# Column-tiled matmuls and a weight matrix turned by DMA in a fused attention and feed-forward kernel

## The chip, the cores and the metric

The kernel runs on one core of one Trainium2 chip. The metric is device time in microseconds (us). The time of a kernel is the median of its runs. A run whose time is over 1.5% above the fastest run of the same kernel counts as slow and is left out of ratios. Times inside one execution come from its profile, in us from the start of its span.

## The reference

It is block-sparse attention, followed by a gated feed-forward network (FFN) without a nonlinearity.

```python
# q, k, v: (4 batches, 8 heads, 768, 64); blocks of 32; tokens = 4*768 = 3072
scores = q @ k.T / 8                      # masked by block: band, first/last block, 3 random blocks per row
attn   = softmax(where(mask, scores, -1e9)) @ v
x      = attn, heads side by side         # (3072, 512)
out    = ((x @ w1) * (x @ w2)) @ w3 @ w_out
# w1, w2: 512x1024; w3: 1024x1024; w_out: 1024x512
```

The kernel multiplies `w3 @ w_out` once (the "fold", tile `wp`) and uses the product for all tokens. The matmuls of this program, on TensorE (PE), take both operands with the summed index on their partitions, so the fold needs w3 turned (`w3t_sb`). Their results go to PSUM tiles, from which ACT (ScalarE) or DVE (VectorE) copies them. POOL (GpSimd) issues the loads, and SP (SyncE) the transposes by DMA.

## The kernel before

A small planner in the program puts the PE work into one fixed order ahead of time. It takes work from three queues: scores and q/k transposes (`qk`), attention output and row sums (`pv`), and everything else (`fill`: masks, fold, FFN). The `fill` queue is in order: what stands at its head blocks what stands behind it. These are the parts that matter here.

```python
# attention output o: four heads at once, each in its own 32 columns of the array
for g in range(4):
    i, h = divmod(g, 2)
    nc.tensor.matmul(acc["o"][32*g:32*g+32, part*QT:(part+1)*QT],
                     lhsT=vn[b, 2*Q+i][:, h, kc, 32*part:32*part+32],
                     rhs=e[:, g, k2*QT:(k2+1)*QT], ..., skip_group_check=True)
...
w3pool = pool("w3pool", 4)                       # four buffers for rows of w3
...
def fold_transpose(i, jh):                       # w3 turned on PE, then copied out of PSUM
    def emit(eng):
        tp = box["p"] = ps_f.tile([128, 4, 128], BF16, tag="f", name="w3p")
        for j in range(4):
            nc.tensor.transpose(tp[:, j, :],
                                w3_sb[i][:, (4*jh+j)*128:(4*jh+j+1)*128], ident)
    op, hold = f_op(0.23, emit, [w3_in[i]])
    w3_hold[i].frees = op
    hold.frees = either(0.42, lambda eng: copy(
        eng, w3t_sb[:, 4*jh:4*jh+4, i*128:(i+1)*128], box["p"]), [op])
...
def fold_mm(i, turned_at):                       # the fold: 128x128 stationary, 512 columns
    ...
    nc.tensor.matmul(box["p"], lhsT=w3t_sb[:, j, i*128:(i+1)*128],
                     rhs=wo_sb[:, j, :], start=j == 0, stop=j == NF-1)
...
def pa(f):                                       # first FFN product (pb is the same with w2)
    for c in range(4):
        nc.tensor.matmul(p, lhsT=w1_sb[:, c, f*128:(f+1)*128],
                         rhs=X[i][:, c, :], start=c == 0, stop=c == 3)
...
# q and k of batches 2 and 3 were already turned by DMA, in the middle of the kernel
nc.sync.dma_start_transpose(out=t[:, x, :].rearrange("r (c p) -> r c p", c=C),
                            in_=ns[x].rearrange("p c h d -> p (c h d)"))
```

The softmax here doesn't subtract the row's maximum and nothing guards it: scores larger than these inputs give would overflow.

## Time and profile before

| | before |
|---|---|
| time, median (range, runs) | 262.22 us (262.19 to 263.07, 3) |
| span of the profiled run | 260.9 us |
| PE busy | 248.4 us, 95% |
| first FFN matmul (`pa`) starts at | 61.8 us |
| PE instructions in program order | 5706 |

The lines below are from the profile's page of the kernel before. The first gives busy time, share of the span and instructions of each engine. The rows `PE` and `PEclk` cut the span into 40 slices and give tenths of busy time and of the full PE clock. The `q` lines are DMA queues: packets, megabytes, and the time of the packets as a share of 16 DMA engines. Queue q0 carries what POOL issues (the loads), q1 what SP issues, q8 fetches instructions.

```profile
PE 248.4 (95%) x2819; PEld 127.6 (49%) x2852; DVE 212.3 (81%) x250; ACT 198.8 (76%) x274; POOL 62.7 (24%) x100
...
PE   7999999999999999999999999999999999997994
...
PEclk9999999999999999999999999999999999999999
...
q1 hardware_dynamic: 17344, 10.88, 16.3%
q8 instruction: 22, 0.36, 0.6%
```

PE is busy in nearly every slice, and always at full clock. So PE bounds the kernel, and the questions are what its time consists of and whether the start, the only place with holes, can be packed more tightly.

The same run by stages: length, busy us and count of each engine, granted clock, DMA share (the time of all packets over that of 16 engines; packets overlap, so it can pass 1), and GB/s.

```profile
core 0: us, PE busy (x) PEld busy (x) DVE busy (x) ACT busy (x) POOL busy (x), PEclk, DMA share, GB/s
20.00:40.00 20.00, 19.00 (x271) 10.41 (x272) 16.26 (x22) 16.78 (x24) 5.90 (x10) 1.00 0.74 121
40.00:60.00 20.00, 18.27 (x259) 9.88 (x260) 16.55 (x19) 18.21 (x27) 16.27 (x27) 1.00 1.18 194
60.00:85.00 25.00, 24.52 (x322) 13.20 (x320) 21.52 (x27) 21.16 (x31) 14.39 (x19) 1.00 1.57 151
```

DMA is not full from 20 to 40 us. The waits of POOL show why: it can't start a load of w3 (`w_...`) before PE has turned an earlier part out of one of the four buffers (`w3p`). The columns are the total wait, how often, and the longest.

```profile
POOL w_722 L367 <- PE w3p L624: 5.3, 1, 5.3
POOL w_613 L367 <- PE w3p L624: 4.8, 1, 4.8
```

The timeline of PE in mid-kernel shows what a change of the array's mode costs. Columns: start, length of the group, the group.

```profile
150.15 0.61 PE L496 MATMUL s<-qkt 64*128 64x256 bf16 x8
150.69 1.50 PE L552 MATMUL o<-e,vn 128*32 128x256 bf16 x48
152.01 0.39 PE L564 MATMUL d<-sum,ones 128*32 128x256 bf16 x8
152.33 1.04 PE L661 MATMUL pa<-x,w_sb 128*128 128x512 bf16 x3
```

Ends are modelled, so starts are read. The row sums `d` (eight 32-column matmuls, two groups of 0.109 us) start at 152.01 and the 128-column `pa` starts 0.32 us later: about 0.1 us more than the streaming. That is a mode change. The step from `o` to `d`, both in 32 columns, has none: 48 matmuls are 12 groups, 12 x 0.109 = 1.31 us, and 152.01 - 150.69 = 1.32 us.

### The profile page before, as it was taken

Reading aid. Unit: us, or ns where it says so; the run is one execution under the profiler, and the core shown is the slowest. Engines: PE = TensorE matmul, PEld = TensorE weight load, DVE = VectorE, ACT = ScalarE, POOL = GpSimd, SP = SyncE. Lnnn points to the kernel's source line nnn. Section 1 sums busy time; section 2 is a strip of 40 time slices with the busy share of each in tenths; the row PEclk is TensorE's granted clock in tenths of the full one; section 3 lists DMA queues with packets and bytes.
Section 4 is the critical chain, followed back from the end, with each engine's and each line's share of the span. In section 5 each row is a group of like instructions: output and inputs, shape, how many; then the busy total and the mean of one; then the engine's idle time right before and its main releaser. Section 6 shows DMA issues by size and latency. Waiting matters only on the chain.

```text
span 260.9 us, 6636 instructions
## 1 busy us (share of the span) xinstructions
PE 248.4 (95%) x2819; PEld 127.6 (49%) x2852; DVE 212.3 (81%) x250; ACT 198.8 (76%) x274; POOL 62.7 (24%) x100
## 2 busy tenths in 40 slices
PE   7999999999999999999999999999999999997994
PEld 4444544554555445554555455545554555453441
DVE  5498789688977978999879988799988799945751
ACT  4789869988887898979899897999879989501000
POOL 8603138698356050009260000000000000000000
PEclk9999999999999999999999999999999999999999
DMA  6999639999989299119999000300002100031013
GB/s 222 163 200 202 104 52 172 206 204 184 164 124 140 60 173 130 33 33 101 164 214 171 3 1 17 124 25 3 0 3 93 72 4 0 3 121 43 0 41 121
DMA packets 53730, 25.34 MB, mean 97 GB/s; under 512 B 39236, under 2 KB 48708, under 8 KB 53700
## 3 DMA queue, kind: packets, MB, share of 16 engines
q0 software_dynamic: 36176, 13.90, 45.9%
q1 hardware_dynamic: 17344, 10.88, 16.3%
q8 instruction: 22, 0.36, 0.6%
q10 hardware_dynamic: 180, 0.13, 0.2%
q14 instruction: 8, 0.07, 0.1%
HBM read 29.36 MB, written 6.29 MB: 137 GB/s over the span
## 4 chain that ended last, share of the span: by engine, by line
PE 86%; DVE 5%; ACT 3%; DMA 2%; issue 2%; SPq 1%
PE pb L678 17%; PE po L699 16%; PE pa L661 16%; PE s L496 14%; PE o L552 13%; PE wp L642 4%; DMA raw<-in_k_dram 2%; DVE e L509 2%; PE d L564 2%; PE tp L399 2%; ACT e L504 2%; PE mp L476 1%; DVE x L604 1%; PE w3p L624 1%; SPq L251 1%
## 5 line engine op out<-in xcount | busy, mean ns | idle before, releaser
L504 ACT ACTIVATE e<-s 128x1024 bf16<-128x1024 f32 x144 | 141.5, 1028 | 14.8 <-PE s L496 14.8
L509 DVE TENSOR_TENSOR e<-e,mask 128x1920 bf16<-128x1920 bf16 x72 | 82.9, 1154 | 16.7 <-ACT e L504 15.7
L661 PE MATMUL pa<-x,w_sb 128*128 128x512 bf16 x175 | 47.6, 380 | 2.6 <-DVE x L604 1.3
L678 PE MATMUL pb<-x,w_sb 128*128 128x512 bf16 x190 | 49.3, 380 | 0.2
L496 PE MATMUL s<-qkt 64*128 64x256 bf16 x576 | 46.9, 279 | 0.7 <-ACT e L504 0.5
L699 PE MATMUL po<-wf_sb,h 128*128 128x512 bf16 x186 | 43.4, 380 | 0.7 <-issue 0.6
L552 PE MATMUL o<-e,vn 128*32 128x256 bf16 x1152 | 38.0, 278 | 1.2 <-DVE x L604 1.0
L496 PEld LDWEIGHTS <-qkt 64*128 64x128 bf16 x576 | 22.5, 96 | 30.7 <-issue 27.8
L684 DVE TENSOR_TENSOR h<-pb,a 128x512 bf16<-128x512 f32 x48 | 33.0, 687 | 4.5 <-PE pb L678 2.0
L552 PEld LDWEIGHTS <-vn 128*32 128x32 bf16 x1152 | 28.5, 98 | 9.6 <-issue 8.4
L535 DVE TENSOR_TENSOR sum<-e 128x2048 bf16<-128x2048 bf16 x24 | 29.3, 1222 | 0.7
L538 DVE TENSOR_TENSOR sum<-sum,e 128x2048 bf16<-128x2048 bf16 x24 | 29.3, 1222 | 0.5
L699 PEld LDWEIGHTS <-h 128*128 128x128 bf16 x192 | 17.6, 98 | 22.3 <-issue 3.2
L678 PEld LDWEIGHTS <-w_sb 128*128 128x128 bf16 x192 | 17.5, 98 | 22.1 <-issue 3.2
L661 PEld LDWEIGHTS <-w_sb 128*128 128x128 bf16 x192 | 16.7, 98 | 23.2 <-issue 6.7
L302 ACT CAST a<-pa 128x512 bf16<-128x512 f32 x36 | 21.2, 588 | 2.4 <-PE pa L661 1.5
L429 POOL DMA_DIRECT2D nt<-in_q_dram x16 | 13.2, 830 | 22.4 <-DMA qkt<-nt 14.6
L595 ACT ACTIVATE ln<-d 128x256 f32<-128x256 f32 x24 | 9.4, 392 | 11.9 <-PE d L564 11.9
L604 DVE TENSOR_TENSOR x<-o,rec 128x512 bf16<-128x512 f32 x24 | 16.4, 684 | 1.8 <-ACT rec L599 1.8
L336 POOL DMA_DIRECT2D vn<-in_v_dram x16 | 11.6, 727 | 24.2 <-PE o L552 20.4
L707 ACT COPY ob<-po 128x256 f32<-128x256 f32 x1 | 0.4, 372 | 21.3 <-PE po L699 21.3
L642 PE MATMUL wp<-wo_sb,w3t_sb 128*128 128x512 bf16 x56 | 15.6, 380 | 0.7 <-issue 0.5
(79 smaller groups left out, 170.0 us busy)
## 6 DMA issues: line engine op xcount, KB each, us to landing
out_dram<-ob SPq DMA_DIRECT2D x23, 256.0 KB, 2.0
vn<-in_v_dram POOLq DMA_DIRECT2D x16, 192.0 KB, 6.0
w_sb<-in_moe_w_dram POOLq DMA_DIRECT2D x16, 128.0 KB, 5.0
nt<-in_q_dram POOLq DMA_DIRECT2D x16, 96.0 KB, 4.5
nt<-in_k_dram POOLq DMA_DIRECT2D x16, 96.0 KB, 5.1
qn<-in_q_dram POOLq DMA_DIRECT2D x6, 192.0 KB, 6.1
kn<-in_k_dram POOLq DMA_DIRECT2D x6, 192.0 KB, 6.4
wo_sb<-in_moe_w_out_dram POOLq DMA_DIRECT2D x1, 1024.0 KB, 13.3
```

The lines of the kernel that those rows point to most:

```text
L302: (nc.scalar.copy if eng == "ACT" else nc.vector.tensor_copy)(dst, src)
L496: nc.tensor.matmul(s[:, h, k2 * QT:(k2 + 1) * QT], lhsT=qk[64 * h:64 * h + 64, 1, kc * 128:(kc + 1) * 128], rhs=qk[64 * h:64 * h + 64, 0, ...
L504: nc.scalar.activation(E[key][:, 2 * i:2 * i + 2, :], box["s"], AF.Exp, scale=1.0 / 8.0)
L509: nc.vector.tensor_tensor(e, e, m.to_broadcast((128, 4, 4, 120)), op=ALU.mult)
L535: nc.vector.tensor_tensor(box["sum"], E[es[0]], E[es[1]], op=ALU.add)
L538: nc.vector.tensor_tensor(box["sum"], box["sum"], E[es[2]], op=ALU.add)
L552: nc.tensor.matmul(acc["o"][32 * g:32 * g + 32, part * QT:(part + 1) * QT], lhsT=vn[b, 2 * Q + i][:, h, kc, 32 * part:32 * part + 32], rhs ...
L642: nc.tensor.matmul(box["p"], lhsT=w3t_sb[:, j, i * 128:(i + 1) * 128], rhs=wo_sb[:, j, :], start=j == 0, stop=j == NF - 1)
L661: nc.tensor.matmul(p, lhsT=w1_sb[:, c, f * 128:(f + 1) * 128], rhs=X[i][:, c, :], start=c == 0, stop=c == 3)
L678: nc.tensor.matmul(p, lhsT=w2_sb[:, c, f * 128:(f + 1) * 128], rhs=X[i][:, c, :], start=c == 0, stop=c == 3)
L684: nc.vector.tensor_tensor(box["h"][:, f, :], box["pb", f], box["a", f], op=ALU.mult)
L699: nc.tensor.matmul(box["o", n], lhsT=box["h"][:, f, n * 128:(n + 1) * 128], rhs=wf_sb[:, f, :], start=f == 0, stop=f == NF - 1)
```

## The change

The intent: let all PE work except scores and transposes run in one mode (four tiles of 32 columns), so that FFN, o and d can follow one another without a change; take the turning of w3 off PE, ACT and DVE and give it to the DMA; and pack the start more tightly (eight w3 buffers, FFN work in pieces of two instead of four matmuls, w1 and w2 loaded before the second batch, new planner constants). The core of the diff, with the cuts marked:

```diff
-    w3pool = pool("w3pool", 4)
-    nat = pool("nat", 4)
+    NW = 8
+    w3pool = pool("w3pool", NW)
+    nat = pool("nat", 8)
 ...
+    def quarters(to, lhsT, rhs, start, stop):
+        for g in range(4):
+            nc.tensor.matmul(to[32 * g:32 * g + 32], lhsT=lhsT[:, 32 * g:32 * g + 32], rhs=rhs,
+                             start=start, stop=stop, skip_group_check=True)
 ...
     def load_w3(lo, hi):
 ...
+            def turn(eng, i=i):
+                dma_at[0] += 1.0
+                nc.sync.dma_start_transpose(out=w3t_sb[:, :, i * 128:(i + 1) * 128], in_=w3_sb[i])
+            hold.frees = w3t_at[i] = plan.add(Op("SP", 1.7, turn, [w3_in[i]], lat=2.0))
 ...
-    def fold_transpose(i, jh):                   # all of it
 ...
+    STEP = 2
+    def chain(name, n, one, deps):               # fold, pa, pb and po all go through this
+        box, hold, ops = {}, Hold(), []
+        for lo in range(0, n, STEP):
+            def emit(eng, lo=lo):
+                if lo == 0:
+                    box["p"] = ps_f.tile([128, 512], F32, tag="f", name=name)
+                for j in range(lo, lo + STEP):
+                    lhsT, rhs = one(j)
+                    quarters(box["p"], lhsT, rhs, j == 0, j == n - 1)
+            ops.append(Op("PE", 0.215 * STEP, emit, deps(lo), [] if ops else [(F_SLOTS, hold)],
+                          "c", lat=0.2))
+        return ops, hold, box
 ...
     tps = {(0, pr): transposes(0, pr) for pr in range(4)}
-    load_pair(1, 0)
-    load_pair(1, 1)
     w1_in = load_w12(moe_w1, w1_sb)
     w2_in = load_w12(moe_w2, w2_sb)
-    load_pair(1, 2)
-    load_pair(1, 3)
+    for pr in range(4):
+        load_pair(1, pr)
+        plan.turn.extend(transposes(1, pr))
```

The mask matmuls also contract over 128 rows instead of 24, and the masks, o, d, fold and FFN share one mode name, "c", in the planner.

## The prediction

> **What bounds it now.** TensorE. The page has PE busy 95% of a 260.9 us span at full clock, DVE 81%, ACT 76%; the chain of waits is 86% PE. Starts of neighbouring matmuls in the timeline: 0.216 us per 128x512 FFN or fold matmul; 0.109 us per group of four 32-column matmuls over 256 columns (o, d) and per pair of scores; 0.056 us per w3 transpose. Times the counts in the program order: 219.7 us of streaming (576 FFN 124.3, 64 fold 13.8, o 31.4, scores 31.4, d 5.2, q/k transposes 7.4, w3 transposes 3.7, masks 2.3).
>
> On top come changes of array mode. FFN to scores starts 312 ns apart instead of 216, FFN to o 309, d to FFN or scores 205 instead of 107, scores to o 199: 93 to 99 ns each. The order has 206 changes: 20.0 us. The Trainium skill ("TensorEngine Tiling (Array Packing)", Key Properties) says that changing the mode drains TensorE; the trace agrees, with about 97 ns.
>
> First useful matmul 4.8 us, last one ends 3.6 us before the end. So 260.9 - 4.8 - 3.6 - 219.7 - 20.0 = 12.8 us are holes: about 10.6 before the first pa (61.8 us), 1.5 near 236 us (pa waits for the last x), almost none between 62 and 230.
>
> **What the change does.**
> - FFN, fold, masks as four 32-column matmuls: estimated from o's rate, 0.216 us per four of 512 columns: no change. PE instructions rise from 5706 to 9786, but eight per 0.216 us is half o's issue rate. The same page (Restrictions) says column tiling turns Fast Weight Load off; in the trace loads take 97 ns either way and hide.
> - FFN-o-d no longer switch mode. But scores stand between most of them: the order after has 175 changes, 31 fewer, 3.0 us; mostly early (68 to 46 before the first pa), in the middle only 136 to 129.
> - w3 by DMA: minus 64 PE transposes (3.7 us) and 16 evictions (0.42 us DVE, 0.59 us ACT). Plus eight DMA transposes; those of 192 KB took 1.2 to 1.4 us to issue and 2.5 to 7 us to land; estimate 1.7 us of all 16 engines and 6 us latency each. Eight w3 buffers end POOL's waits for w3p (12 us), with DMA half idle (28 to 40 us).
> - The last o and d now stand before 30 po matmuls: the hole near 236 us goes.
> - The first FFN may start after 29 score units, not 33; w1/w2 load before batch 1.
>
> **On the critical path.** All PE savings count, if holes do not grow: 4.8 + 216.0 + 17.0 + 3.6 + holes = 241.4 us + holes. Until the first pa, PE has 37 us of work after its start at 4.8, ACT is busy to about 49 us (29 x 1.03 plus copies), and w2 lands at 50 to 54 us (6.8 MB at the 0.2 MB/us seen, plus transposes). So 9 to 11 us of holes stay. Span 251.5, time about 1 more.
>
> **Prediction: 252.5 us, range 248.5 to 257.5.** Faster by over 2% 0.87, within 2% 0.12, slower 0.01.
>
> **What would show it.** FFN groups 0.216 us apart; d to pa without the 97 ns; first pa at 49 to 54 us; no hole before the last FFN; PE busy still 95%; ACT and DVE some 4 us less each.
>
> **What would make it wrong.** Four-tile groups slower than 0.216 us (1% is 1.4 us); instruction fetch falling behind; w3 transposes landing late, so that the in-order fold blocks the FFN behind it (5 us or more); or early loads so much better that holes fall to 5 us (247).

## The result and the profile after

| | before | after |
|---|---|---|
| time, median (range, runs) | 262.21 us (261.93 to 263.07, 4) | 292.13 us (288.43 to 295.39, 4, one of them slow) |
| ratio of fast runs | 1 | 1.109 (95% interval 1.098 to 1.120) |
| span of the profiled run | 260.9 us | 286.7 us |
| first `pa` at | 61.8 us | 84.7 us |
| mean granted PE clock | 0.998 | 0.944 |

A ratio here is the mean time of one kernel's fast runs over the mean of the other's in the same rounds, so it is not quite the ratio of the medians. The first three runs before are those of the table above. The kernel is 11% slower; 252.5 us was predicted. The profiled run (288.43 us) was a fast one.

The page after, the lines that answer to those before:

```profile
PE 251.8 (88%) x4892; PEld 133.8 (47%) x4892; DVE 211.8 (74%) x250; ACT 189.9 (66%) x259; POOL 62.9 (22%) x100
...
PE   6775714965589999999999999999999999999994
...
PEclk9795975797799999999999999999999999999998
...
q1 hardware_dynamic: 25792, 12.98, 28.7%
q8 instruction: 38, 0.62, 0.9%
```

The PE row has holes in its first twelve slices and is full from then on. The clock row has holes in the same place. Queue q1 carries 8448 packets and 2.10 MB more: the eight transposes of 256 KB, as 8192 packets of 256 bytes and 256 of 4 bytes. By stages, in the same columns as before:

```profile
20.00:40.00 20.00, 10.85 (x184) 5.06 (x176) 10.82 (x12) 6.88 (x10) 6.91 (x13) 0.82 1.25 178
40.00:60.00 20.00, 12.37 (x196) 5.96 (x200) 5.39 (x7) 7.19 (x10) 7.39 (x13) 0.67 1.26 110
60.00:85.00 25.00, 15.68 (x256) 7.50 (x252) 10.55 (x12) 12.06 (x18) 5.73 (x8) 0.86 1.30 128
85.00:150.00 65.00, 64.41 (x1304) 34.65 (x1300) 58.53 (x65) 60.40 (x84) 22.50 (x29) 1.00 1.05 95
```

Before 85 us PE, DVE and ACT do less than in the kernel before, PE partly at a lower clock. DMA is now full nearly all the time. It moves more from 20 to 40 us (178 GB/s instead of 121), but less from 40 to 60 us, 110 GB/s where it was 194, and this includes the w3 pieces. What PE waited for:

```profile
PE wp L299 <- DMA w3t_sb<-w_336: 9.9, 1, 9.9
PE wp L299 <- DMA w3t_sb<-w_511: 4.5, 1, 4.5
PE wp L299 <- DMA w3t_sb<-w_268: 4.5, 1, 4.5
...
PE wp L299 <- DMA w3t_sb<-w_546: 2.0, 1, 2.0
PE wp L299 <- DMA w3t_sb<-w_583: 1.9, 1, 1.9
```

Seven waits of the fold for a w3 transpose make 24.8 us (the five longest are shown). The timeline of PE shows the longest wait, and what such a wait costs afterwards:

```profile
35.56 1.48 PE L299 MATMUL wp<-wo_sb,w3t_sb 128*32 128x512 bf16 x24
46.93 1.04 PE L299 MATMUL wp<-wo_sb,w3t_sb 128*32 128x512 bf16 x8 [9.89 <-DMA w3t_sb<-w_336]
...
67.11 3.40 PE L299 MATMUL wp<-wo_sb,w3t_sb 128*32 128x512 bf16 x32 [4.50 <-DMA w3t_sb<-w_511]
70.44 0.61 PE L517 MATMUL s<-qkt 64*128 64x256 bf16 x8
```

The 32 matmuls from 67.11 us are eight groups of four. They take 70.44 - 67.11 = 3.33 us, where 8 x 0.216 = 1.73 us is the rate at full clock. The Trainium skill ("TensorE: Matmul & The Clock Gate", HAM oscillation) says that gaps of more than about 3.4 us make the clock fall to half; this trace agrees, with a group of four at 0.42 us after a gap of 4.5 us. But shorter gaps did it too: in this trace half clock also followed a gap of 2.0 us that began at 71.0 us, and in experiment 1 a stall of 2.0 us.

The DMA-issuing side, the timeline of SP. The length is that of the issuing instruction.

```profile
12.33 1.33 SPq L384 DMA_TRANSPOSE w3t_sb<-w_268  x1
19.77 1.89 SPq L384 DMA_TRANSPOSE w3t_sb<-w_313  x1
21.70 4.01 SPq L384 DMA_TRANSPOSE w3t_sb<-w_336  x1
28.68 11.82 SPq L384 DMA_TRANSPOSE w3t_sb<-w_440  x1
```

The transpose behind the 9.9 us wait was issued at 21.7 us and its user could start at 46.9 us: 25 us. Its successor kept SP busy for 11.8 us in issue alone.

What follows is, in its rates, what was predicted. The timeline of PE after 150 us:

```profile
151.16 0.62 PE L299 MATMUL po<-wf_sb,h 128*32 128x512 bf16 x8
151.60 1.49 PE L573 MATMUL o<-e,vn 128*32 128x256 bf16 x48
...
179.71 0.39 PE L585 MATMUL d<-sum,ones 128*32 128x256 bf16 x8
179.93 0.60 PE L299 MATMUL pb<-x,w_sb 128*32 128x512 bf16 x8
```

Two FFN groups of four tiles take 151.60 - 151.16 = 0.44 us, so a group costs 0.22 us, as much as one 128-column matmul before, and there is no extra step into `o`. From `d` to `pb` it is 0.22 us for two groups of 0.109 us: no mode change, where it was 0.32 us.

### The profile page after: what moved, and what is told of

It reads as the page before. It is cut to its first block, busy times and chain, and to the rows that moved or that the text cites. A ratio compares the mean times of both kernels' runs of the same rounds, so it can differ in the third digit from the quotient of the medians.

```text
span 286.7 us, 10729 instructions
## 1 busy us (share of the span) xinstructions
PE 251.8 (88%) x4892; PEld 133.8 (47%) x4892; DVE 211.8 (74%) x250; ACT 189.9 (66%) x259; POOL 62.9 (22%) x100
## 3 DMA queue, kind: packets, MB, share of 16 engines
q0 software_dynamic: 36176, 13.90, 48.9%
q1 hardware_dynamic: 25792, 12.98, 28.7%
## 4 chain that ended last, share of the span: by engine, by line
PE 69%; DMA 24%; POOL 3%; ACT 1%; DVE 1%; issue 1%; POOLq 0%
PE pb L299 15%; PE pa L299 15%; PE po L299 14%; PE s L517 11%; PE o L573 10%; DMA w3t_sb<-w_583 7%; DMA w_sb<-in_moe_w_dram 7%; DMA qn<-in_q_dram 5%; DMA w_511<-in_moe_w_dram 5%; PE d L585 2%; PE tp L416 1%; ACT e L525 1%; PE wp L299 1%; POOL vn L345 1%; POOL A L281 0%
## 5 line engine op out<-in xcount | busy, mean ns | idle before, releaser
L530 DVE TENSOR_TENSOR e<-e,mask 128x1920 bf16<-128x1920 bf16 x72 | 82.7, 1153 | 21.7 <-ACT e L525 21.4
L299 PEld LDWEIGHTS <-w_sb 128*32 128x32 bf16 x1536 | 37.5, 96 | 39.4 <-issue 6.5
L299 PE MATMUL pb<-x,w_sb 128*32 128x512 bf16 x768 | 51.8, 380 | 0.0
L299 PE MATMUL pa<-x,w_sb 128*32 128x512 bf16 x768 | 51.1, 380 | 0.0
L299 PE MATMUL po<-wf_sb,h 128*32 128x512 bf16 x768 | 45.2, 380 | 0.0
L299 PE MATMUL wp<-wo_sb,w3t_sb 128*32 128x512 bf16 x256 | 22.3, 493 | 24.8 <-DMA w3t_sb<-w_336 9.9
L573 PEld LDWEIGHTS <-vn 128*32 128x32 bf16 x1152 | 30.1, 99 | 7.6 <-issue 4.3
L299 PEld LDWEIGHTS <-h 128*32 128x32 bf16 x768 | 19.3, 97 | 20.0 <-issue 2.5
L299 PEld LDWEIGHTS <-w3t_sb 128*32 128x32 bf16 x256 | 6.9, 114 | 35.2 <-DMA w3t_sb<-w_336 10.4
L316 ACT CAST a<-pa 128x512 bf16<-128x512 f32 x33 | 19.5, 591 | 3.4 <-PE pa L299 3.3
## 6 DMA issues: line engine op xcount, KB each, us to landing
kn<-in_k_dram POOLq DMA_DIRECT2D x6, 192.0 KB, 14.3
```

The lines of the kernel that those rows point to most:

```text
L299: nc.tensor.matmul(to[32 * g:32 * g + 32], lhsT=lhsT[:, 32 * g:32 * g + 32], rhs=rhs, start=start, stop=stop, skip_group_check=True)
L316: (nc.scalar.copy if eng == "ACT" else nc.vector.tensor_copy)(dst, src)
L530: nc.vector.tensor_tensor(e, e, m.to_broadcast((128, 4, 4, 120)), op=ALU.mult)
L573: nc.tensor.matmul(acc["o"][32 * g:32 * g + 32, part * QT:(part + 1) * QT], lhsT=vn[b, 2 * Q + i][:, h, kc, 32 * part:32 * part + 32], rhs ...
```

## The experiments

Theory A was: the DMA transposes of w3 arrive late, and the in-order fold holds up everything behind it. The rivals were: B, the split of each matmul into four (instruction count, column tiles) makes PE slow; C, the new order of loads and the planner's order of work does it. Once A stood, the question became why the transposes are late: A1, the turning itself is slow; E, the transfer's many small pieces are slow beside the loads, turned or not. The experiments are numbered in the order of the argument, and "kernel 1" is the kernel of experiment 1; the names in brackets are those that the expectations use (e8, e9, e10 and e11 are experiments 7 to 10). The diff of each is against the kernel named. Experiments 1 to 4 ran on one chip, 5 to 8 on a second and 9 and 10 on a third, each beside runs of the kernel before on the same chip. A kernel of one run is compared by what its trace shows and by differences far above 2%.

### 1. The change with w3 turned on PE again (e1_pe_w3)

```diff
 (against after)
-            def turn(eng, i=i): ... nc.sync.dma_start_transpose(...)
+    def fold_transpose(i, jh): ...               # as before, one mode of its own; feeds w3t_at[i]
```

> The changed kernel with w3 turned on TensorE again (64 transposes, 16 evictions) and nothing sent through the DMA crossbar for it; column tiles, pieces of two, batch order, load order and eight w3 buffers stay. Theory A (the w3 transposes in the DMA queues, late among the loads, hold up the in-order fold and with it all else, and nothing else in the change costs anything): no hole longer than 3 us on PE before the first pa, clock near 1.0, first pa at 53 to 60 us, time 253 to 260 us. Rival B (column tiles or the new plan cost the time, the wait for w3 only hides it): time stays above 270 us. Rival C (the clock throttle in the first 87 us is caused by something else than the idle PE): clock stays near 0.94.

Measured: 260.21 us (257.16 to 261.82, four runs), ratio to before 0.989 (0.982 to 0.996). The first `pa` was at 61.0 us and w2 had landed at 42.6 us instead of 66.6. The time and the first `pa` are at the edge of what was expected, 0.2 and 1.0 us above it. So without the DMA turning the 30 us are gone; B and C, with all of their parts still in this kernel, fall as causes of it.

The gain over before is smaller than the prediction wanted, even so. The profiled run (the slowest of the four) has two stalls that no tile, semaphore or slot explains: 0.8 us, ending at 81.5 us, and 2.0 us, ending at 140.3 us; half clock follows the second for 3.4 us.

### 2. The same, with 128-column matmuls again (e2_pe_w3_full)

```diff
 (against 1)
     def quarters(to, lhsT, rhs, start, stop):
-        for g in range(4):
-            nc.tensor.matmul(to[32 * g:32 * g + 32], lhsT=lhsT[:, 32 * g:32 * g + 32], rhs=rhs, ...)
+        nc.tensor.matmul(to, lhsT=lhsT, rhs=rhs, start=start, stop=stop)
```

> As e1, but every group of four 32-column matmuls of FFN, fold, masks and warming is one 128-column matmul again, in the same order. This measures the column tiles alone. The order has 213 changes of mode against 182: if a change costs 97 ns here too, 3.0 us slower than e1; if the tiles are of no use 0; if four-tile groups stream slower than one matmul, e2 is faster than e1.

Measured: 258.60 us (258.06 to 259.62, four runs), ratio 0.988 (0.985 to 0.991), and no unexplained stall in its trace (here and below: none over 0.5 us). It should have been 3.0 us slower than kernel 1, for the mode changes that it has more, and was not: a miss. It has only 22 instruction fetches instead of 38. The column tiles' gain is given back somewhere; experiments 7, 8 and 10 look for it.

### 3. Before, with only the DMA turning (e3_before_dma_w3)

```diff
 (against before)
+            def turn(eng, i=i):
+                nc.sync.dma_start_transpose(out=w3t_sb[:, :, i * 128:(i + 1) * 128], in_=w3_sb[i])
+            hold.frees = w3t_at[i] = plan.add(Op("SP", 1.7, turn, [w3_in[i]], lat=2.0))
-    def fold_transpose(i, jh): ...
 ...
```

> The kernel before with w3 turned by the DMA crossbar and nothing else of the change (four w3 buffers as before, so the loads behind w3 wait for the transposes). Theory A: slower than before, 270 to 295 us, with PE waiting for w3t and first pa later than 75 us. If the transposes only hurt together with the new load order or with eight buffers: 255 to 265 us.

Measured: 288.07 us (one run), as expected under theory A. PE waited 13.1 us for `w3t_sb`:

```profile
PE wp L633 <- DMA w3t_sb<-w: 13.1, 4, 4.9
```

The first `pa` moved from 61.8 to 89.9 us. So this one part, put into the old kernel, costs 25.8 us of its own, most of the loss of 29.9. It needs neither eight buffers nor the new load order nor column tiles.

### 4. The change, with a fold that doesn't wait for the turning (e4_fold_unturned)

This computes a wrong result: the transposes still run, but the fold reads w3 unturned.

```diff
 (against after)
-        ops, hold, box = chain("wp", NF, lambda j: (w3t_sb[:, j, i * 128:(i + 1) * 128], wo_sb[:, j, :]),
-                               lambda j: [w3t_at[i], wo_in])
+        ops, hold, box = chain("wp", NF, lambda j: (w3_sb[i][:, j * 128:(j + 1) * 128], wo_sb[:, j, :]),
+                               lambda j: [w3_in[i], wo_in])
```

> The changed kernel with all DMA transposes still running, but the fold reads w3 as loaded, not turned (wrong result on purpose). Separates the two ways in which the transposes can hurt. If only the wait of the fold hurts: 250 to 256 us, first pa near 52 us. If the transposes also slow the loads beside them (w2 landed at 66 us in the changed kernel): PE waits for w1, w2 or q, k instead, first pa at 62 to 70 us, time 262 to 272 us.

Measured: 282.60 us (one run), so outside what was expected; only 6 to 10 us of the loss was won back. The first `pa` came at 56.5 us, but then PE waited 14.3 us for the q of the second batch, and w2 landed at 70.7 us.

```profile
PE tp L416 <- DMA qn<-in_q_dram: 14.3, 1, 14.3
```

Unexplained stalls of PE, as in kernel 1, took 8.0 us more, the longest 3.2 us. The theory "the fold's wait is the loss" is therefore too narrow. The transposes also slow the loads beside them, and when the fold doesn't wait for the one, PE waits for the other.

### 5. Two w3 buffers instead of eight (e5_two_w3_buffers)

```diff
 (against after)
-    NW = 8
+    NW = 2
```

> The changed kernel with two buffers for w3 rather than eight: a load of w3 waits for the transpose before last, and POOL, in order, issues nothing behind it, so the later transposes run with few loads beside them. If loads beside it are what makes a transpose slow: transposes 4 to 6 of w3 land 3 to 8 us after issue (12 to 21 us in the changed kernel), w2 lands at 60 to 70 us, time 265 to 278 us. If a w3 transpose is slow by itself: they still take 10 us or more, and the time is 290 us or more.

Measured: 277.61 us (one run, correct), within what was expected. Here the loads of w3 wait for the transposes, so some transposes run with few loads beside them. This is the last line of the trace's view of the tile `w3t_sb` (for seven of the eight transfers; the landing of the fourth is not in the view), first after the change, then with two buffers:

```profile
DMA to landing us min/median/max: 12.3/19.1/25.2
```

```profile
DMA to landing us min/median/max: 3.0/7.8/11.7
```

Transposes issued at 19.4, 40.8 and 43.1 us, with few loads in flight, landed after 3.0, 3.5 and 4.9 us. Those issued at 48.9 and 52.6 us, beside the loads of w1 and w2, took 7.9 and 11.7 us; the one at 25.6 us, beside loads of q, k and v, took 11.2. So the latency depends on what runs beside a transpose. The 2.5 to 7 us from which the prediction took its 6 us had been measured in mid-kernel, on smaller transposes.

### 6. Plain copies in place of the transposes (e6_plain_copy)

This computes a wrong result: the same bytes in the same 1024 pieces of 256 bytes, not turned.

```diff
 (against after)
-                nc.sync.dma_start_transpose(out=w3t_sb[:, :, i * 128:(i + 1) * 128], in_=w3_sb[i])
+                nc.sync.dma_start(out=w3t_sb[:, :, i * 128:(i + 1) * 128],
+                                  in_=w3_sb[i].rearrange("p (j c) -> p j c", c=128))
```

> The changed kernel, with each of the eight DMA transposes of w3 replaced by a plain DMA copy on the same queue, of the same 256 KB, also cut into pieces of 256 bytes (w3 is then not turned: wrong result on purpose). Same plan, same order. Theory A1 (it is the crossbar transposes that get and leave little bandwidth beside loads): copies land within 4 us, w2 lands before 50 us (66 us in the changed kernel, 42 us in e1), time 250 to 258 us. Rival A2 (any 2 MB more on the queues, in pieces of 256 bytes, would do it): copies land after 10 us or more, time 275 to 290 us.

Measured: 277.87 us (one run), in the range of rival A2 of the expectation. The copies landed as late as the transposes:

```profile
DMA to landing us min/median/max: 12.1/18.8/25.3
```

PE waited 17.6 us for them. So A1 alone falls: a plain copy in such pieces is just as late. The turning adds something else: w2 landed at 49.5 us here, at 66.6 us with transposes, and at 42.6 us with neither. From 40 to 60 us all traffic together is 200 GB/s, not 110:

```profile
40.00:60.00 20.00, 15.79 (x269) 7.70 (x273) 8.11 (x8) 11.92 (x16) 11.14 (x17) 0.81 1.24 200
```

So the small pieces come late by themselves, but it takes the turning to slow the loads this much.

### 7. The q/k transposes of later batches as plain copies (e8_qk_plain_copy)

This is wrong in q and k of batches 2 and 3. The check of correctness nevertheless passed, so passing says nothing here. The copies are also not in the same pieces, as the expectation has it: queue q1 carried 6848 packets instead of 17344, with the same 10.88 MB, because no piece of 256 bytes is left (the copies go in pieces of 1536 bytes). So the run takes away the turning and the small pieces together.

```diff
 (against 1)
-                nc.sync.dma_start_transpose(out=t[:, x, :].rearrange("r (c p) -> r c p", c=C),
-                                            in_=ns[x].rearrange("p c h d -> p (c h d)"))
+                nc.sync.dma_start(out=t[:, x, :].rearrange("r (c p) -> r c p", c=C),
+                                  in_=ns[x].rearrange("p c h d -> p c (h d)"))
```

> e1 (w3 on PE, column tiles), with the q and k transposes of batches 2 and 3 replaced by plain DMA copies in the same pieces (wrong result on purpose). e1 showed a stall of 2.4 us on PE at 137.7 us that no wait explains, beside an instruction fetch of 2.5 us and a q/k transpose, and then 3.4 us at half clock. Theory D (column tiles need 38 instruction fetches instead of 22, and a fetch beside a DMA transpose can come late): no unexplained stall over 0.5 us between 100 and 215 us, clock 0.993 or more, 254 to 257 us. Rival: such stalls stay.

Measured: 257.11 us (256.72 and 257.51), ratio 0.982 (0.971 to 0.994). There was no unexplained stall after 60 us, with the same number of PE instructions as kernel 1. From the first `o` to the end this run was 3.0 us shorter than kernel 2, which is what 31 mode changes at 0.097 us make. Its start was about 2.4 us longer than kernel 2's, in part because its clock was still low until 13.8 us, against 6.7. So the column tiles seem to save what was predicted, where nothing takes it away. Kernel 2 still had its q/k transposes, so this comparison isn't clean; experiment 10, which has them too, gives a second one.

### 8. As many instructions, but no column tiles (e9_split_columns)

Each 128-column matmul is cut into four along the moving columns: the stationary operand stays whole, and there are 9842 PE instructions.

```diff
 (against 1)
+        w = to.shape[-1] // 4
         for g in range(4):
-            nc.tensor.matmul(to[32 * g:32 * g + 32], lhsT=lhsT[:, 32 * g:32 * g + 32], rhs=rhs, ...)
+            nc.tensor.matmul(to[:, g * w:(g + 1) * w], lhsT=lhsT, rhs=rhs[:, g * w:(g + 1) * w], ...)
```

> e1 with the FFN, fold and mask matmuls over all 128 columns of weights, each cut into four along the moving columns instead (4 x 128, or 4 x 64 for the masks): as many PE instructions as e1 (9842), but no column tiles. Theory D: unexplained stalls and drops of the clock as in e1, though there are no tiles. Streaming by the rate of the w3 transposes (0.056 us for 128 columns) 0.224 us for 512, 5 us more in all than e2, and more if the four weight loads do not hide: 262 to 275 us.

Measured: 264.39 us (263.99 and 264.78), ratio 1.010 (0.998 to 1.022). The result was wrong (relative error 0.67), which was not intended. So only its timing is used. The waits of PE for "issue", time in which it waited for nothing that the profile shows:

```profile
PE pb L299 <- issue: 1.1, 1, 1.1
PE s L510 <- issue: 0.8, 1, 0.8
```

They end at 140 and 81 us, as in kernel 1, in a kernel without column tiles for this work. So the stalls don't need the tiles. The drop of the clock that was also expected did not come. What the stalls do need is taken up under the point on instruction fetch, below.

### 9. The plain copies in pieces of 2 KB (e10_copy_2k)

This is wrong, as kernel 6: the same bytes, in 128 pieces of 2 KB.

```diff
 (against 6)
-                nc.sync.dma_start(out=w3t_sb[:, :, i * 128:(i + 1) * 128],
-                                  in_=w3_sb[i].rearrange("p (j c) -> p j c", c=128))
+                nc.sync.dma_start(out=w3t_sb[:, i, :], in_=w3_sb[i])
```

> As e6 (a plain copy on the same queue in place of each w3 transpose, wrong result on purpose), but each copy in 128 pieces of 2 KB instead of 1024 of 256 bytes; bytes, queue, plan and order are the same. In e6 the copies landed 12 to 22 us after issue. Theory E (on each of the 16 engines a piece of the copy waits for about one 2 KB packet of the loads, so the number of pieces sets the time: 64 pieces at about 0.2 us in e6, 8 here): copies land in 3 to 6 us, wp no longer waits over 1 us, w2 lands before 50 us, time 250 to 257 us. Rival (the bytes or the queue set it): copies still land after 10 us or more, time 270 us or more.

Measured: 258.95 us (one run), 19 us shorter than kernel 6, but 2 us above the 250 to 257 us that were expected.

```profile
DMA to landing us min/median/max: 6.4/6.9/7.9
```

The landings were expected within 3 to 6 us, so that is a miss by one to two microseconds; but they are less than half of the 18.8 us of the same bytes in small pieces. The first `pa` came at 52.1 us, inside the 49 to 54 us that the prediction gave for the change. PE waited for `w3t_sb` 1.9 us in all, once for 1.7 us, where none over 1 us was expected. w2 landed at 48.5 us, only 1 us before kernel 6's. The stage from 40 to 60 us:

```profile
40.00:60.00 20.00, 19.08 (x404) 11.02 (x396) 17.26 (x19) 18.68 (x26) 14.55 (x21) 1.00 1.25 203
```

PE is busy 19.08 us, instead of 15.79 in kernel 6 and 12.37 after the change, at full clock. With no small pieces and no turning the start of the change comes out as predicted. The whole doesn't: 258.95 us is 1.5 us above the predicted range, and this trace has 2.4 us of unexplained stalls. Theory E stands: between kernels 6 and 9 only the pieces (and the chip) differ, and the copies' latency falls from 18.8 to 6.9 us.

How the small pieces lose is seen in the packets of the two queues in the same 12 us, from 28 to 40 us. First after the change, then kernel 6, then kernel 1, in which no w3 transposes run, then this kernel. The columns are packets, MB, and share of 16 engines; q0 are the loads, q1 the w3 pieces.

```profile
q0 software_dynamic: 1196, 1.78, 92.2%
q1 hardware_dynamic: 1498, 0.37, 27.8%
```

```profile
q0 software_dynamic: 1280, 2.04, 91.4%
q1 hardware_dynamic: 1568, 0.39, 22.4%
```

```profile
q0 software_dynamic: 1420, 2.39, 110.1%
```

```profile
q0 software_dynamic: 1142, 1.90, 85.4%
q1 hardware_dynamic: 543, 1.01, 24.9%
```

After the change 1498 pieces went through beside 1196 load packets: about one and a quarter per load packet, though a piece is a sixth of a load packet's bytes. A transpose is 1024 pieces, 64 for each of 16 engines; 1498 / 16 in 12 us is one piece of an engine in 0.128 us, so 8.2 us for one transpose while the loads run (an estimate from these counts), and a transpose that is issued behind another waits for it too. Kernel 6, not turned, is alike: 1568 beside 1280. In pieces of 2 KB the same 12 us took 1.01 MB of copies instead of 0.37 and 0.39. The Trainium skill ("DMA: Bandwidth & Descriptors", Queues, rings and completion order) says that each DMA engine takes turns between the queues that have work, packet by packet. The page's packet is a bundle of descriptors, while a packet of the trace is one piece. The counts fit such turns: what a queue gets goes by the number of pieces rather than by bytes. They don't show how many descriptors a turn holds.

### 10. Kernel 1, with column tiles only before 58 and after 146 us (e11_tiles_late)

If the stalls come with many PE instructions while q/k transposes run, whole matmuls should be used in just that stretch.

```diff
 (against 1)
-    def quarters(to, lhsT, rhs, start, stop):
+    def quarters(to, lhsT, rhs, start, stop, whole=False):
+        if whole:
+            nc.tensor.matmul(to, lhsT=lhsT, rhs=rhs, start=start, stop=stop)
+            return
 ...
+                    box["whole"] = 58.0 < plan.free["PE"] < 146.0
```

> An attempt at a version that beats both: e1 (w3 on PE, column tiles), but FFN chains that the plan starts between 58 and 146 us, where q/k transposes of batches 2 and 3 run on the DMA queues, use whole 128-column matmuls. 8402 PE instructions (9842 in e1, 5762 in e2), 194 changes of mode (182 and 213). If the theory of late instruction fetches holds: no unexplained stall over 0.5 us, about 1.8 us below e2 by the changes of mode, 255 to 258 us, ratio to before 0.975 to 0.985. If stalls come all the same: 258 to 261 us.

Measured: 257.38 us (255.88 to 257.79, six runs; correct), before in the same rounds 262.63 us (eleven runs), ratio 0.980 (0.976 to 0.984), as expected. There is no unexplained stall over 0.5 us, and there are 33 instruction fetches. From the first `o` to the end it is 2.2 us shorter than kernel 2, where 19 mode changes fewer at 0.097 us make 1.8. It is faster than both kernels, by 2.0% over before; the interval doesn't settle whether the gain is above 2%.

## Why the prediction was wrong

**The step that failed** is the costing of the eight w3 transposes: "estimate 1.7 us of all 16 engines and 6 us latency each", and what was built on it: "w2 lands at 50 to 54 us (6.8 MB at the 0.2 MB/us seen, plus transposes)" and "9 to 11 us of holes stay". The terms were mis-sized:

- Latency: 12.3, 19.1 and 25.2 us (shortest, median, longest) instead of 6 us. It had been taken from mid-kernel transposes of 192 KB; in the trace before, those with no loads beside them landed after 2.5 to 2.6 us, the others after 4.5 to 7.0. Experiment 5 shows that it depends on the loads beside, experiments 6 and 9 that it depends on the number of pieces.
- The DMA time: queue q1 took 28.7% of 286.7 us of 16 engines instead of 16.3% of 260.9 us. That is 39.8 us more, or 5.0 us for each of the eight transposes instead of 1.7 (an estimate: packets overlap, and other traffic of the queue got longer too).
- The loads: all DMA traffic together, pieces included, was 110 GB/s from 40 to 60 us, where the prediction reckoned with 0.2 MB/us (200 GB/s) for the loads and experiment 9 has 203; w2 landed at 66.6 us. The small pieces alone don't do this: kernel 6 has them, with 200 GB/s and w2 at 49.5 us. It is the turning.
- The clock: not in the sum at all. With PE waiting, it was granted 0.82, 0.67 and 0.86 of full clock from 20 to 85 us.

Together these moved the first `pa` from the predicted 49 to 54 us to 84.7 us. What failed is thus the overlap: the prediction's sum has no wait of the fold for the transposes, and the in-order fold waited 24.8 us for them. The kernel without turning and with large pieces (experiment 9) has the same work before the first `pa` and reaches it at 52.1 us: 32.6 us less. The waits for `w3t_sb` are 24.8 - 1.9 = 22.9 us of that. The remaining 9.7 us hold the work at half clock and smaller waits; they were not separated further. By the spans of the profiled runs, taking away the turning (kernel 6) saves 286.7 - 276.1 = 10.6 us, and large pieces (kernel 9) save 276.1 - 257.2 = 18.9 us more. These are single runs on three chips, on which the kernel before had medians of 262.2 to 262.6 us.

The prediction did name this failure: "w3 transposes landing late, so that the in-order fold blocks the FFN behind it (5 us or more)". So the mechanism was known and only its size was wrong: the waits came to 24.8 us, and the kernel is 29.9 us slower. The chance of slower, 0.01, was far too low for a term whose only measurement came from another stage.

Point by point:

- "FFN groups 0.216 us apart": right, 0.22 us in the timeline.
- "d to pa without the 97 ns": right; 0.22 us from d to pb, where 0.32 us was seen before. The Trainium skill ("TensorEngine Tiling (Array Packing)", Key Properties) says that a change of the mode, not of the tile, drains TensorE; here the mode is kept, and the trace shows no such step.
- "31 fewer" mode changes, 3.0 us: supported by experiment 7, where the stretch from the first o to the end is 3.0 us shorter (with the q/k transposes gone too), and by experiment 10 (2.2 us for 19 changes). In kernel 1 unexplained stalls of 2.9 us and half clock after one of them took it back.
- "First pa at 49 to 54 us": wrong, 84.7 us; reached, at 52.1 us, without the turning and the small pieces.
- "No hole before the last FFN": right; PE is busy 35.00 of 35 us from 220 us on.
- "PE busy still 95%": wrong, 88%.
- "ACT and DVE some 4 us less each": ACT is 8.9 us less busy, DVE only 0.5 us.
- "Instruction fetch falling behind": listed as a risk, and a candidate for the second, smaller loss. The traces are these. With 38 fetches and q/k transposes, stalls over 0.5 us appear in kernels 1, 4, 5, 8 and 9, but not after the change and not in kernel 6. With 22 fetches (before, kernels 2 and 3), with 33 (kernel 10), or with 38 and no q/k transposes (kernel 7, one trace, the small pieces gone too), there are none. So many PE instructions and the transposes together are not enough for a stall; that both are needed fits these traces, but is not shown. In kernel 1's profiled run, its slow one, the fetch beside the second stall took 2.5 us, where the median of its fetches is 1.1 us. But its fetch at 44 us took 2.1 us without a stall, and in kernel 8, a fast run, the fetch beside a like stall took 1.1 us. That a late fetch is the cause is argued, not shown.

What stays open: why the turning slows the loads more than a plain copy in the same pieces does, and what exactly PE waits for in the stalls. Both kernel 2 and kernel 10 turn w3 on PE and beat the kernel before; kernel 2 has no column tiles in the FFN, so most of kernel 10's 5.2 us over before seems to come from the order of loads and work (kernel 2 has 3.6 us of medians without those tiles, on another chip), not from the tiles.

## What to carry to other kernels

A DMA's latency from one stage of a kernel says little about another: before moving work to the DMA, ask what else uses the engines then, and count the pieces of the transfer, not its bytes. A transfer in 256-byte pieces beside loads of mostly 2 KB packets arrived late here, and a turned one slowed the loads as well; give it an idle stretch, large pieces, or leave the work on an engine that has it at a known cost (here 3.7 us of PE). If work in an in-order queue may wait for such a transfer, cost the wait together with the low clock that follows it.

## What the Trainium skill lacked or had wrong

- "DMA: Bandwidth & Descriptors", Latency and other measured facts: it gives 261 GB/s as the effective bandwidth of a DMA transpose, measured on one kernel. Beside loads, the w3 transposes here moved 0.37 MB in 12 us, 31 GB/s (plain copies in the same pieces 0.39 MB, so this is not the turning); with few loads beside, 256 KB landed in 3.0 us, 87 GB/s with the latency in it. The page has no time for a transpose beside loads: here 3.0 us against 12 to 25 us.
- The same page, Rules for kernel authors: it says that a transpose next to ordinary DMAs needs nothing. That is about safety, and the results here were right; in time, all DMA traffic together was 110 GB/s from 40 to 60 us with the transposes and 200 GB/s with the same bytes copied in the same pieces, which no page tells.
- "Runtime: NRT & Kernel Launch", Instruction fetch mechanics: it says that instructions come in blocks of 16 KiB (256 instructions) and that crossing a block is mostly hidden. The first agrees: 5706 PE instructions and 22 fetches, 9786 and 38. To the second: five of seven kernels with 38 fetches and DMA transposes of q and k had PE stalls over 0.5 us (kernel 8: 0.8 and 1.1 us), which the three with 22 did not; whether the fetch is the cause was not settled.
- "TensorEngine Tiling (Array Packing)": it has no time at which groups of four column tiles over 512 columns, each group doing one full matmul, follow one another, and no other page has it. It is 0.22 us per group of four, the same as one 128-column matmul.
